# Decode attention over a long cache: softmax with a running maximum per head

## The chip, the cores and the metric

The kernel runs on one core of a Trainium2 chip. The metric is device time in microseconds (us) of one execution; the kernel before has a median of 1265.78 us over three runs (1265.28 to 1266.05).

## What is computed

One token is decoded. A gate `g` mixes the result of an attention block with that of a small MLP ("mixer"). The attention has 16 query heads on 8 key/value heads (so two query heads share each cache head), 65,536 cached positions and a head size of 256, all in bf16:

```python
scores = jnp.einsum("bhqd,bhkd->bhqk", q, k) * (Dh ** -0.5)
p = _softmax(scores, axis=-1)
o = jnp.einsum("bhqk,bhkd->bhqd", p, v)
return (lambda x, *d: x.transpose(*d))(o, 0, 2, 1, 3).reshape(B, Sq, Hq * Dh) @ wo
...
g = _sigmoid((x * gate_w).sum(-1, keepdims=True))
a = _A_ref(x, A_k_cache, A_v_cache, A_wq, A_wo)
b = _B_ref(x, B_w1, B_b1, B_w2, B_b2)
return g * a + (1 - g) * b
```

The two caches are 268 MB each. Each element of them is read once.

## The kernel before

**Tiling.** The 8 cache heads (`H`) are cut into 4 load pairs each (`PPH`), 32 in all (`NP`), numbered j = 0 to 31 here. A pair is one load of 8 MiB of K and one of 8 MiB of V, 16,384 positions, as 128 partitions x 128 positions x 256. A pair is worked through in 8 blocks (`BODY`) of 16 tiles of 128 positions (`NT`). K lives in a ring of one and a half pairs (`kring`), V in one buffer (`vbuf`). The last pair's K comes as two halves, its V as four pieces.

**DMA queue.** SP issues every large load, in order (L239 to L263): for each pair the K load, once half the transposes of the pair before are done (L242), then the V load, once the values of the pair before are done (`sem_pv`, L255), and in the first pair of heads 1 to 6 that head's output weights `wo_sb` (L263), once the projection with the old ones is done (L262). After the last pair the final two parts of `wo_sb` follow (L265 to L268).

**Keys (TensorE).** For each block `transposes` (L301) turns 16 tiles of K, read as 32-bit words, into four PSUM banks `kst`; DVE copies two of the banks to `ktT` (L572) and ACT the other two (L672). `scores` (L321) then multiplies each tile by the two queries in `qcur`: 32 small matmuls of two columns per block, into one of two PSUM banks of `sps`, by the parity of the block. TensorE runs the transposes of a block ahead of the scores of the block before it.

**Weights (ACT).** After each block of scores ACT takes the exponential of the bank's 32 columns, scaled, into `pT` (L661), with no maximum subtracted. TensorE waits for it before it overwrites the bank (L315).

**Values (TensorE).** After the eight blocks of a pair, `values` waits for the last exp (L348), adds the eight blocks of `pT`, summed over partitions by a matmul with ones, to the denominators (`acc[:, DENC:SELC]`, L350), then runs 128 matmuls of `pT` columns with `vbuf` (L361), which add to `acc[:, 0:DENC]` at rows 0, 32, 64 and 96 in turn. `acc` is one PSUM bank, and gathers over the four pairs of a head. In the last pair four projections (L345) and eight matmuls without a use (`spin(8)`, L337) stand ahead of L348, and the values from 112 on go through `late_values` (L382) into `sps[:, 0, 0:4]`.

**End of a head.** DVE copies `acc` out (`take`, L578), TensorE clears it and gathers the four row groups (`by_row`, L397), DVE scales by the reciprocal denominators and TensorE projects with `wo_sb` (L408).

**Mixer.** In pairs 0 to 13 DVE computes one tile of the MLP after its evacuations (L547 to L565, with a tanh on ACT, L678), and TensorE adds four small matmuls after the values (L471).

All order between engines is by semaphores written out by hand; each engine works through its own instructions in order.

Of the kernel before, what the change touches and what calls it, by code (L numbers as in the profile page):

```python
# [8 lines left out]
ALU = mybir.AluOpType  # L9
# [3 lines left out]
def bass_gated_mix__gqa_block_cached__mixer_token_mlp__decode_kernel(  # L13
# [57 lines left out]
    assert WG * NCG == DM  # L71

    scale = 1.0 / (DH ** 0.5)
    GC0 = 0.796875
    GC1 = 0.044677734375

# [15 lines left out]
    with ctx:  # L92
        def sb(shape, dt, name):
            return ctx.enter_context(nc.sbuf_tensor(name, shape, dt))

        def psum(shape, dt, name):
            return ctx.enter_context(nc.psum_tensor(name, shape, dt))
# [51 lines left out]
        sel = sb([P, REP], f32, "sel")  # L149
        zrow = sb([1, NACC], bf16, "zrow")  # L150
        rden = sb([P, REP], f32, "rden")
        densum = sb([P, REP], f32, "densum")
        rrow = sb([P, 1], f32, "rrow")
        b2_b = sb([1, 1], bf16, "b2_b")
# [15 lines left out]
        kst = psum([P, NB, 512], f32, "kst")  # L170
        kst_b = kst.bitcast(bf16)
        sps = psum([P, 2, 512], f32, "sps")
        acc = psum([P, 512], f32, "acc")
        prj = psum([P, 512], f32, "prj")

# [12 lines left out]
        sem_qk = new_sem("sem_qk")  # L188
        sem_exp = new_sem("sem_exp")
        sem_pv = new_sem("sem_pv")  # L190
        s_par = new_sem("s_par")
        s_hb = new_sem("s_hb")
        s_sel = new_sem("s_sel")
# [91 lines left out]
        def _(pe):  # L285
# [26 lines left out]

            def scores(k, c):
                par = k % 2
                pe.wait_ge(sem_exp, c + 1)  # L315
                for nt in range(NT):
                    b, ntl = divmod(nt, 4)
                    if k == BODY - 1 and ntl == 0:
                        pe.wait_ge(sem_ev[b], c + 2)
                    for dj in range(2):  # L320
                        ins = pe.matmul(sps[:, par, 2 * nt:2 * nt + 2],  # L321
                                        ktT[:, par, b, ntl * DH + dj:(ntl + 1) * DH:2],
                                        qcur[:, dj, :],
                                        start=(dj == 0), stop=(dj == 1))
                ins.then_inc(sem_qk, 1)
# [11 lines left out]
                    pe.matmul(kst[:, NB - 1, :], ones_sq[:, :], ktT[:, KTB - 1, 0, 0:512], start=True, stop=True)  # L337


            def values(j, c0, u16):  # L340
                with pe.If(j == NP - 1):
                    pe.wait_ge(s_mix, 1)
                    for q in range(NCG):
                        r = slice(32 * q, 32 * q + 1)
                        pe.matmul(prj[r, 0:WG], rest[r, :], brow[r, :], start=False, stop=True,  # L345
                                  skip_group_check=True)
                    spin(8)
                pe.wait_ge(sem_exp, c0 + (BODY + 2))  # L348
                for r in range(BODY):
                    pe.matmul(acc[:, DENC:SELC], ones_sq[:, :], pT[:, r, :],  # L350
                              start=False, stop=(r == BODY - 1), skip_group_check=True)

                def some(n0, n1, last=False):
                    if last:
                        piece_wait(n0)
                    else:
                        pe.wait_ge(sem_v, u16)
                    for n in range(n0, n1):
                        r, nt = divmod(n, NT)
                        o = 32 * (n % 4)  # L360
                        ins = pe.matmul(acc[o:o + REP, 0:DH], pT[:, r, 2 * nt:2 * nt + 2], vbuf[:, n, :],  # L361
                                        start=False, stop=False, skip_group_check=True)
# [14 lines left out]
            def late_values(n0, n1):  # L377
                for n in range(n0, n1):
                    r, nt = divmod(n, NT)
                    piece_wait(n)  # L380
                    for dj in range(2):
                        ins = pe.matmul(sps[:, 0, dj * REP:(dj + 1) * REP], vbuf[:, n, dj:DH:2],  # L382
                                        pT[:, r, 2 * nt:2 * nt + 2], start=False,
                                        stop=(n == NV - 1), skip_group_check=True)
                return ins
# [27 lines left out]

            def tail():
                pe.wait_ge(s_cp, H)
                by_d(sps[:, 0, 0:2 * REP])
# [66 lines left out]
        def _(vec):  # L483
            for b in range(0, NB, 2):
                vec.sem_inc(sem_ev[b], 1)
            vec.memset(xrem, 0.0)
            vec.memset(zrow[:, :], 0.0)
            vec.wait_ge(sem_ident, 1)
            vec.tensor_copy(identb, ident[0:3 * FT, 0:3 * FT]).then_inc(s_xrem, 1)
            vec.reduce_sum(sel[:, :], ident[:, :].rearrange("p (j n) -> p n j", j=4)[:, 0:REP, :], axis=AX.X)  # L490
# [102 lines left out]

            def finish_head(g):
                take(vec.snap(g * PPH + PPH, min_val=PPH, max_val=NP))
                vec.tensor_copy(qcur[:, :, :], qT[:, :, bass.ds(g * REP + REP, REP)])
# [32 lines left out]
            with nc.Fori(NC - NCPH, NC, BODY, engines=on) as c0:  # L629
                for k in range(BODY):  # L630
                    evacuate(k, c0 + k)
            take(1, s_early)
            vec.wait_ge(s_late, 1)
            by_head(sps[:, 0, 0:2 * REP])
# [5 lines left out]
        def _(act):  # L640
# [6 lines left out]
            act.sem_inc(sem_exp, 2)  # L647
# [18 lines left out]
            with nc.Fori(0, NP, 1, engines=OrderedEngineSet([act.engine])) as j:  # L666
                c0 = act.snap(j * BODY, min_val=0, max_val=NC)
                for k in range(BODY):
                    act.wait_ge(sem_qk, c0 + (k + 1))
                    for b in range(1, NB, 2):  # L670
                        act.wait_ge(sem_tr[b], c0 + (k + 1))
                        act.activation(ktT[:, k % KTB, b, :], kst_b[:, b, :], AF.Copy).then_inc(sem_ev[b], 1)  # L672
                    if k >= 1:
                        weights(k - 1, c0 + (k - 1))
                weights(BODY - 1, c0 + (BODY - 1))
                with act.If(j < FT):
                    act.wait_ge(s_u, j + 1)
                    act.activation(z_b[:, :], z_b[:, :], AF.Tanh).then_inc(s_tanh, 1)  # L678
# [32 lines left out]
```

## Time and profile before

| what | us |
|---|---|
| runs (median of 3) | 1265.78 |
| profiled execution, span | 1263.6 |
| TensorE matmul busy | 920.2 (73%) |
| ACT busy | 536.8 (42%) |
| DVE busy | 422.5 (33%) |
| share of 16 DMA engines in use | 99.7% |
| rate of the loads, mean | 431 GB/s |

The span is that of one profiled execution; the median of the runs stands 2.2 us above it. The costliest groups of instructions, each with its count, then its busy time, the mean of one in ns, and the idle time of its engine just before it with what ended it:

```profile
L672 ACT ACTIVATE ktT<-kst 128x1024 bf16<-128x1024 bf16 x512 | 498.5, 1021 | 668.1 <-PE kst L301 667.8
L301 PE MATMUL kst<-ident,kring 128*128 128x128 f32 x4096 | 554.2, 296 | 301.5 <-DMA kring<-in_A_k_cache_dram 289.8
L572 DVE COPY ktT<-kst 128x1024 bf16<-128x1024 bf16 x512 | 354.2, 692 | 762.8 <-PE kst L301 738.8
L321 PE MATMUL sps<-qcur,ktT 128*128 128x2 bf16 x8192 | 236.6, 163 | 1.1 <-issue 1.1
L361 PE MATMUL acc<-vbuf,pT 128*2 128x256 bf16 x4080 | 153.7, 323 | 3.4 <-issue 2.9
L661 ACT ACTIVATE pT<-sps 128x32 f32 x256 | 52.3, 204 | 16.2 <-PE sps L321 16.2
```

Matmuls overlap, so the mean length of one times their count is more than their busy time: the busy time is what the group took from the engine.

### The profile page before, as it was taken

The page shows a single profiled execution, that of the slowest core. Times are in us where ns is not written, and L with a number is a line of the kernel's source. Part 1 is how long each engine was busy: PE and PEld are TensorE (multiplying, and loading weights), DVE is VectorE, ACT ScalarE, POOL GpSimd, SP SyncE. Part 2 cuts the span into 40 slices and gives each one's busy share as a digit, 9 for nine tenths or more (in the row PEclk, how much of TensorE's full clock was granted, in tenths as well). Part 3 has the DMA queues.
Part 4 walks back from the last instruction along what each step waited for, and adds up shares of the span by engine and source line. Part 5 has one row for each costly group of instructions (what it writes and reads, how often), then busy time and mean ns, then how long its engine had stood idle before and what let it go on. Part 6 is the DMA issues. An engine that isn't in the chain of part 4 may idle for free.

```text
span 1263.6 us, 38848 instructions
## 1 busy us (share of the span) xinstructions
PE 920.2 (73%) x17112; PEld 864.9 (68%) x17114; DVE 422.5 (33%) x764; ACT 536.8 (42%) x788; POOL 0.9 (0%) x7
## 2 busy tenths in 40 slices
PE   2876678766778667786676876768767688676788
PEld 2766668766677666686666876658766578666687
DVE  2433344333344234343222332223323133332233
ACT  1543345533355433454333553335533355433455
POOL 0000000000000000000000000000000000000000
PEclk9887788787898887988788887789887888887899
DMA  9999999999999999999999999999999999999998
GB/s 416 430 430 432 434 432 434 436 434 436 432 434 432 432 434 436 425 436 436 438 432 429 432 432 434 436 436 434 432 434 432 440 434 432 432 434 434 432 426 369
DMA packets 11623, 544.39 MB, mean 431 GB/s; under 512 B 1369, under 2 KB 1628, under 8 KB 2908
## 3 DMA queue, kind: packets, MB, share of 16 engines
q1 hardware_dynamic: 11522, 544.22, 99.7%
q8 instruction: 8, 0.13, 0.0%
q10 hardware_dynamic: 90, 0.01, 0.0%
q14 instruction: 3, 0.02, 0.0%
HBM read 544.22 MB, written 0.00 MB: 431 GB/s over the span
## 4 chain that ended last, share of the span: by engine, by line
DMA 71%; PE 28%; issue 1%; SPq 0%; DVEq 0%; DVE 0%; ACT 0%; ACTq 0%
DMA kring<-in_A_k_cache_dram 68%; PE kst L301 23%; PE sps L321 4%; DMA wo_sb<-in_A_wo_dram 2%; PE acc L361 0%; SPq L236 0%; SPq L233 0%; SPq L268 0%; SPq L231 0%; SPq L228 0%; PE acc L350 0%; DVEq L92 0%; PE prj L408 0%; DVE out_row L637 0%; ACT pT L661 0%
## 5 line engine op out<-in xcount | busy, mean ns | idle before, releaser
L672 ACT ACTIVATE ktT<-kst 128x1024 bf16<-128x1024 bf16 x512 | 498.5, 1021 | 668.1 <-PE kst L301 667.8
L301 PE MATMUL kst<-ident,kring 128*128 128x128 f32 x4096 | 554.2, 296 | 301.5 <-DMA kring<-in_A_k_cache_dram 289.8
L301 PEld LDWEIGHTS kst<-ident,kring 128*128 128x128 f32 x4096 | 504.3, 154 | 311.4 <-issue 308.8
L572 DVE COPY ktT<-kst 128x1024 bf16<-128x1024 bf16 x512 | 354.2, 692 | 762.8 <-PE kst L301 738.8
L321 PEld LDWEIGHTS sps<-qcur,ktT 128*128 128x128 bf16 x8192 | 237.8, 96 | 3.9 <-issue 1.4
L321 PE MATMUL sps<-qcur,ktT 128*128 128x2 bf16 x8192 | 236.6, 163 | 1.1 <-issue 1.1
L361 PE MATMUL acc<-vbuf,pT 128*2 128x256 bf16 x4080 | 153.7, 323 | 3.4 <-issue 2.9
L361 PEld LDWEIGHTS acc<-vbuf,pT 128*2 128x2 bf16 x4080 | 111.5, 98 | 37.3 <-issue 3.4
L661 ACT ACTIVATE pT<-sps 128x32 f32 x256 | 52.3, 204 | 16.2 <-PE sps L321 16.2
L350 PE MATMUL acc<-pT,ones_sq 128*128 128x32 bf16 x256 | 11.7, 178 | 12.2 <-ACT pT L661 12.2
L350 PEld LDWEIGHTS acc<-pT,ones_sq 128*128 128x128 bf16 x256 | 8.6, 96 | 15.1 <-ACT pT L661 14.9
L578 DVE COPY accs<-acc 128x288 f32<-128x288 f32 x8 | 3.7, 458 | 40.1 <-PE acc L361 40.1
L678 ACT ACTIVATE z_b<-z_b 128x448 bf16<-128x448 bf16 x14 | 8.1, 576 | 20.7 <-DVE z_b L559 20.7
L397 PEld LDWEIGHTS acc<-sel,accs 128*64 128x64 f32 x112 | 10.8, 214 | 0.9
L397 PE MATMUL acc<-sel,accs 128*64 128x1 f32 x112 | 11.4, 261 | 0.0
L434 PE MATMUL acc<-vbuf 42*128 42x42 bf16 x1 | 0.2, 215 | 8.6 <-DMA b_b<-in_B_b_dram 8.6
L434 PEld LDWEIGHTS acc<-vbuf 42*128 42x128 bf16 x1 | 0.1, 102 | 8.7 <-DMA b_b<-in_B_b_dram 8.7
L408 PE MATMUL prj<-wo_sb,oTn 128*1 128x112 bf16 x128 | 3.5, 230 | 3.4 <-DVE oTn L603 2.9
L553 DVE TENSOR_TENSOR z_b<-wtmp,u_b 128x448 bf16<-128x448 bf16 x14 | 5.5, 393 | 1.0
L551 DVE TENSOR_TENSOR wtmp<-u_b 128x448 bf16<-128x448 bf16 x14 | 5.5, 392 | 1.0
L565 DVE TENSOR_TENSOR gu<-wtmp,z_b 128x448 bf16<-128x448 bf16 x14 | 5.5, 392 | 1.0
L557 DVE TENSOR_TENSOR z_b<-u_b,wtmp 128x448 bf16<-128x448 bf16 x14 | 5.5, 392 | 1.0
(89 smaller groups left out, 81.8 us busy)
## 6 DMA issues: line engine op xcount, KB each, us to landing
kring<-in_A_k_cache_dram SPq DMA_DIRECT2D x4, 4096.0 KB, 24.4
vbuf<-in_A_v_cache_dram SPq DMA_DIRECT2D x1, 6144.0 KB, 25.5
wo_sb<-in_A_wo_dram SPq DMA_DIRECT2D x7, 448.0 KB, 27.2
vbuf<-in_A_wq_dram SPq DMA_DIRECT2D x1, 3072.0 KB, 10.3
vbuf<-in_A_v_cache_dram SPq DMA_DIRECT2D x1, 1024.0 KB, 27.6
vbuf<-in_A_v_cache_dram SPq DMA_DIRECT2D x1, 768.0 KB, 28.7
vbuf<-in_A_wq_dram SPq DMA_DIRECT2D x1, 512.0 KB, 11.1
vbuf<-in_A_v_cache_dram SPq DMA_DIRECT2D x31, 29.5
```

Of the source, the lines that this page charges most:

```text
L301: ins = pe.transpose(kst[:, b, i * P:(i + 1) * P], kring_f[:, at + NT * (k % DC) + 4 * b + i, :], ident[:, :])
L321: ins = pe.matmul(sps[:, par, 2 * nt:2 * nt + 2], ktT[:, par, b, ntl * DH + dj:(ntl + 1) * DH:2], qcur[:, dj, :], start=(dj == 0), stop=(d ...
L350: pe.matmul(acc[:, DENC:SELC], ones_sq[:, :], pT[:, r, :], start=False, stop=(r == BODY - 1), skip_group_check=True)
L361: ins = pe.matmul(acc[o:o + REP, 0:DH], pT[:, r, 2 * nt:2 * nt + 2], vbuf[:, n, :], start=False, stop=False, skip_group_check=True)
L397: ins = pe.matmul(dst[hh * HP:(hh + 1) * HP, i:i + 1], accs[:, i:DH:2 * REP], sel[:, hh:hh + 1], start=False, stop=True, skip_group_check= ...
L551: vec.tensor_tensor(W, U, U, op=ALU.mult)
L553: vec.tensor_tensor(Z, W, U, op=ALU.mult)
L557: vec.tensor_tensor(Z, U, W, op=ALU.add)
L572: vec.tensor_copy(ktT[:, k % KTB, b, :], kst_b[:, b, :]).then_inc(sem_ev[b], 1)
L661: act.activation(pT[:, bass.ds(p0 + k % DC, 1), :].rearrange("p o n -> p (o n)"), sps[:, k % 2, 0:2 * NT], AF.Exp, scale=scale).then_inc(s ...
L672: act.activation(ktT[:, k % KTB, b, :], kst_b[:, b, :], AF.Copy).then_inc(sem_ev[b], 1)
L678: act.activation(z_b[:, :], z_b[:, :], AF.Tanh).then_inc(s_tanh, 1)
```

## The change

The softmax now subtracts a maximum, per query head, that runs along with the load pairs. The scores of all eight blocks of a pair go side by side into one PSUM bank (`scores_all`, 256 columns: block, tile, head), and the exps wait until the whole pair's scores are there. TensorE no longer waits for an exp between blocks.

Once per pair, between scores and values, this happens in order. DVE takes the maximum over the tiles of each partition and head (128x256 to 128x2) and the larger of that and the running maximum; TensorE transposes the 128x2 result to 2x128 (`mxT`); DVE takes the maximum of each row and sets it on a 2x2 diagonal; TensorE multiplies that with ones, which puts both maxima on all 128 partitions (`mxB`); DVE makes the bias `mneg` and the difference `mdif` between the old and the new maximum; ACT takes the exponential of the difference, `fade`, and then four exps, each of 64 columns (half of the blocks, one head), with `mneg` as bias, into `pT`; DVE meanwhile multiplies the denominators and the sums in `acc`, in PSUM, by `fade`; TensorE waits for both before it goes on to the denominators. At the end of a head the running maximum is set back to a very low value. The late values of the last pair go to the second bank of `sps`.

```diff
             def scores(k, c):
                 par = k % 2
-                pe.wait_ge(sem_exp, c + 1)
...
-                        ins = pe.matmul(sps[:, par, 2 * nt:2 * nt + 2],
+                        ins = pe.matmul(sps[:, 0, 2 * (NT * k + nt):2 * (NT * k + nt) + 2],
...
+            def maxima(j1):
+                pe.wait_ge(s_mcol, j1)
+                pe.transpose(mxT, mcol[:, :], ident[:, :]).then_inc(s_mT, 1)
+                pe.wait_ge(s_mdiag, j1)
+                pe.matmul(mxB, mones[:, :], mdiag[:, :], start=True, stop=True).then_inc(s_mB, 1)
...
             def values(j, c0, u16):
+                j1 = pe.snap(j + 1, min_val=1, max_val=NP)
+                maxima(j1)
                 with pe.If(j == NP - 1):
...
-                pe.wait_ge(sem_exp, c0 + (BODY + 2))
+                pe.wait_ge(s_acc, j1)
+                pe.wait_ge(sem_exp, j1)
...
+            vec.memset(mones[:, :], 1.0)
+            vec.memset(mrun[:, :], LOW)
...
+            def maxima(j1, c0):
+                vec.wait_ge(sem_qk, c0 + (BODY + 2))
+                vec.tensor_reduce(out=mcol[:, :], in_=scores_all.rearrange("p (n hh) -> p hh n", hh=REP),
+                                  axis=AX.X, op=ALU.max)
+                vec.drain()
+                vec.tensor_tensor(mcol[:, :], mcol[:, :], mrun[:, :], op=ALU.max).then_inc(s_mcol, 1)
+                vec.wait_ge(s_mT, j1)
+                vec.tensor_reduce(out=mrow[:, :], in_=mxT, axis=AX.X, op=ALU.max)
+                vec.drain()
+                vec.tensor_scalar(mdiag[:, :], ident[0:REP, 0:REP], mrow[:, :], None, op0=ALU.mult
+                                  ).then_inc(s_mdiag, 1)
+                vec.wait_ge(s_mB, j1)
+                vec.tensor_scalar(mneg[:, :], mxB, -scale, None, op0=ALU.mult)
+                vec.tensor_tensor(mdif[:, :], mrun[:, :], mxB, op=ALU.subtract).then_inc(s_mneg, 1)
+                vec.drain()
+                vec.tensor_copy(mrun[:, :], mxB)
+                vec.wait_ge(s_fade, j1)
+                vec.tensor_tensor(acc[:, DENC:SELC].rearrange("p (n hh) -> p n hh", hh=REP),
+                                  acc[:, DENC:SELC].rearrange("p (n hh) -> p n hh", hh=REP),
+                                  fade[:, :].rearrange("p (o hh) -> p o hh", o=1).broadcast_to((P, NT, REP)),
+                                  op=ALU.mult)
+                vec.tensor_tensor(fadej[:, :], fade[:, :], sel[:, :], op=ALU.mult)
+                vec.drain()
+                vec.reduce_sum(fader[:, :], fadej[:, :], axis=AX.X)
+                vec.drain()
+                vec.tensor_scalar(acc[:, 0:DENC], acc[:, 0:DENC], fader[:, :], None, op0=ALU.mult
+                                  ).then_inc(s_acc, 1)
...
                     for k in range(BODY):
                         evacuate(k, c0 + k)
+                    maxima(vec.snap(j + 1, min_val=1, max_val=NP), c0)
                     with vec.If(j < FT):
                         mixer(j)
...
-            def weights(k, c):
-                p0 = act.snap(pt_reg, min_val=0, max_val=DC)
-                act.wait_ge(sem_qk, c + 3)
-                act.activation(pT[:, bass.ds(p0 + k % DC, 1), :].rearrange("p o n -> p (o n)"),
-                               sps[:, k % 2, 0:2 * NT], AF.Exp, scale=scale).then_inc(sem_exp, 1)
-                if k == DC - 1:
-                    act.reg_sub(pt_reg, DC, pt_reg)
+            def weights(j1):
+                act.wait_ge(s_mneg, j1)
+                act.activation(fade[:, :], mdif[:, :], AF.Exp, scale=scale).then_inc(s_fade, 1)
+                for half in range(2):
+                    p0 = act.snap(pt_reg, min_val=0, max_val=DC)
+                    for hh in range(REP):
+                        ins = act.activation(pT[:, bass.ds(p0, DC), hh:2 * NT:REP],
+                                             scores_all.rearrange("p (a r n hh) -> p a hh r n", a=2, r=DC, hh=REP)[:, half, hh],
+                                             AF.Exp, bias=mneg[:, hh:hh + 1], scale=scale)
+                    if half == 0:
+                        act.reg_sub(pt_reg, DC, pt_reg)
+                ins.then_inc(sem_exp, 1)
...
-                    if k >= 1:
-                        weights(k - 1, c0 + (k - 1))
-                weights(BODY - 1, c0 + (BODY - 1))
+                weights(act.snap(j + 1, min_val=1, max_val=NP))
```

More of the change, by code (lines that the diff above doesn't have):

```diff
@@ L73, in bass_gated_mix__gqa_block_cached__mixer_token_mlp__decode_kernel @@
     scale = 1.0 / (DH ** 0.5)
+    LOW = -3.0e38
     GC0 = 0.796875
@@ L151, in bass_gated_mix__gqa_block_cached__mixer_token_mlp__decode_kernel @@
         rden = sb([P, REP], f32, "rden")
+        mrun = sb([P, REP], f32, "mrun")
+        mcol = sb([P, REP], f32, "mcol")
+        mrow = sb([REP, 1], f32, "mrow")
+        mdiag = sb([REP, REP], f32, "mdiag")
+        mones = sb([REP, P], f32, "mones")
+        mneg = sb([P, REP], f32, "mneg")
+        mdif = sb([P, REP], f32, "mdif")
+        fade = sb([P, REP], f32, "fade")
+        fadej = sb([P, REP], f32, "fadej")
+        fader = sb([P, 1], f32, "fader")
         densum = sb([P, REP], f32, "densum")
@@ L172, in bass_gated_mix__gqa_block_cached__mixer_token_mlp__decode_kernel @@
         sps = psum([P, 2, 512], f32, "sps")
+        SC = BODY * 2 * NT
+        scores_all = sps[:, 0, 0:SC]
+        mxT = sps[0:REP, 1, 0:P]
+        mxB = sps[:, 1, P:P + REP]
+        late = sps[:, 1, 2 * P:2 * P + 2 * REP]
+        assert SC <= 512
         acc = psum([P, 512], f32, "acc")
@@ L190, in bass_gated_mix__gqa_block_cached__mixer_token_mlp__decode_kernel @@
         sem_pv = new_sem("sem_pv")
+        s_mcol = new_sem("s_mcol")
+        s_mT = new_sem("s_mT")
+        s_mdiag = new_sem("s_mdiag")
+        s_mB = new_sem("s_mB")
+        s_mneg = new_sem("s_mneg")
+        s_fade = new_sem("s_fade")
+        s_acc = new_sem("s_acc")
         s_par = new_sem("s_par")
@@ L381, in late_values @@
                     for dj in range(2):
-                        ins = pe.matmul(sps[:, 0, dj * REP:(dj + 1) * REP], vbuf[:, n, dj:DH:2],
+                        ins = pe.matmul(late[:, dj * REP:(dj + 1) * REP], vbuf[:, n, dj:DH:2],
                                         pT[:, r, 2 * nt:2 * nt + 2], start=False,
@@ L415, in tail @@
                 pe.wait_ge(s_cp, H)
-                by_d(sps[:, 0, 0:2 * REP])
+                by_d(late)
                 late_values(NLATE, NV).then_inc(s_late, 1)
@@ L595, in finish_head @@
                 take(vec.snap(g * PPH + PPH, min_val=PPH, max_val=NP))
+                vec.memset(mrun[:, :], LOW)
                 vec.tensor_copy(qcur[:, :, :], qT[:, :, bass.ds(g * REP + REP, REP)])
@@ L628, in _ @@
             vec.tensor_scalar(brow, brow1, bcast[:, 2:3], None, op0=ALU.add).then_inc(s_mix, 1)
-            with nc.Fori(NC - NCPH, NC, BODY, engines=on) as c0:
+            with nc.Fori(NP - PPH, NP, 1, engines=on) as j:
+                c0 = vec.snap(j * BODY, min_val=0, max_val=NC)
                 for k in range(BODY):
                     evacuate(k, c0 + k)
+                maxima(vec.snap(j + 1, min_val=1, max_val=NP), c0)
             take(1, s_early)
             vec.wait_ge(s_late, 1)
-            by_head(sps[:, 0, 0:2 * REP])
+            by_head(late)
             vec.wait_ge(s_proj, H)
@@ L646, in _ @@
             act.dma_start(b2_b[:, :], B_b2.rearrange("(a n) -> a n", a=1)).then_inc(sem_misc, 16)
-            act.sem_inc(sem_exp, 2)
             for b in range(1, NB, 2):
```

## The prediction

> **What bounds the kernel now.** I read the page of the profile first, its DMA table and the chain that ended last, then the waits of the DMA queue and of TensorE, then the timeline of the last two load pairs.
>
> ```profile
> q1 hardware_dynamic: 11522, 544.22, 99.7%
> ...
> SPq L236 <- PE acc L361: 539.6, 31, 23.9
> ...
> PE kst L301 <- DMA kring<-in_A_k_cache_dram: 289.8, 31, 12.1
> ```
>
> The sixteen DMA engines are never free, and before each pair's transposes (L301) TensorE sits waiting for the K load, 289.8 us in 31 waits. So in the middle of the run compute has slack and the loads set the pace. How much slack: a V load is issued when the values of the pair before are done (SP's wait on L361), and must be issued before the K load ahead of it in the queue has landed. Taking the start of each pair's first transposes as the landing, the 30 V issues up to pair 30 come 9.01 to 12.06 us before it (63.58 against 72.59 is the least, 101.77 against 111.28 the next; mean 10.4). A queue started from nothing needs time: the first load is issued at 0.74, no byte moves by 1.6, the rate is full by 2.8, so I ask for 2.1 us of lead. 6.9 us (least) to 8.3 us (mean) may be lost between scores and values before a load is late.
>
> The end is different. First the chain of waits over the values of pair 30 (start, length, what), then the timeline of pair 31 (in brackets the idle time before):
>
> ```profile
> 1223.45 1.59 PE sps L321 x64
> ...
> 1225.42 0.36 PE acc L350 x8
> 1225.79 3.62 PE acc L361 x128
> ```
>
> ```profile
> 1230.82 3.83 PE L301 MATMUL kst<-ident,kring 128*128 128x128 f32 x32 [1.44 <-DMA kring<-in_A_k_cache_dram]
> ...
> 1241.02 1.96 PE L301 MATMUL kst<-ident,kring 128*128 128x128 f32 x16 [0.42 <-issue]
> ...
> 1250.57 1.74 PE L321 MATMUL sps<-qcur,ktT 128*128 128x2 bf16 x64
> ...
> 1254.13 0.35 PE L350 MATMUL acc<-pT,ones_sq 128*128 128x32 bf16 x8
> 1254.98 3.23 PE L361 MATMUL acc<-vbuf,pT 128*2 128x256 bf16 x112 [0.50 <-DMA vbuf<-in_A_v_cache_dram]
> ```
>
> Pair 30's scores end at 1225.04 and its values at 1229.41. Pair 31's K comes as two halves, so its first half is there 1.41 us later, and from 1230.82 TensorE works almost without a pause to the end: idle 0.42 at the second half, 0.50 at V. The chain of waits names the last wo load (landed 1261.12), but TensorE needs that only 0.19 us after it could have used it (first projection ends 1260.97, second starts 1261.16). Load and TensorE end together; nearly every us lost by TensorE after 1201.74 is a us of the total.
>
> Last, the granted clock, over two runs of pair values and one start of keys:
>
> ```profile
> 680.05:685.38 5.33, 5.33 (x131) 3.69 (x128) 0.00 (x0) 0.00 (x0) 0.00 (x0) 0.68 0.97 418
> ...
> 696.34:702.57 6.23, 6.23 (x39) 6.22 (x40) 2.47 (x4) 2.82 (x3) 0.00 (x0) 0.58 0.90 389
> ...
> 720.50:724.20 3.70, 3.70 (x134) 2.95 (x130) 0.00 (x0) 0.00 (x0) 0.00 (x0) 1.00 0.86 372
> ```
>
> The seventh number is the clock. The same 128 matmuls take 3.67 us at 1.00 and 5.33 at 0.68. In half-microsecond slices the clock is 0.50 from 602.55 to 605.95, and every fall lies a multiple of 3.41 us from this one: the grant is renewed per period. It fell here although only the two-column scores and a 0.39 us gap came before; the period 640.10 to 643.51, with 1.76 us of denominators and values (from 641.75), kept 1.00; the one from 599.13, with some 1.3 us of transposes and values beside the scores, lost it.
>
> **The change, part by part.** *Removed:* eight exps per pair on ACT (0.204 each) and TensorE's wait for them in the scores. A block of keys takes 1.81 (transposes) + 0.78 (scores) = 2.59 us, and TensorE is busy for all of it; ACT uses 2 x 1.02 + 0.20 = 2.24. So this gives nothing; if ACT were the bound it would give up to 0.2 per block.
>
> *Added before the first pair:* two small DVE memsets, 0.17 each by L486, in DVE's 0.53 us idle before L489: nothing, or 0.3 us that the loads cover.
>
> *Added between scores and values of every pair:* a round trip in which nothing overlaps. From the end of the scores:
> - DVE starts, 0.10 (ACT's L661 starts 0.15 after them, L578 0.06 after L361). Maximum of 128x256 from PSUM: no such row; between L580 (32 elements, 0.186) and L497 (448, 0.607) a straight line gives 0.41. Drain gap 0.07 (646.49 to 646.56), running maximum 0.164 (L591). Sum 0.75.
> - TensorE: hand-over 0.12 (L603 ends 648.38, load at 648.50), transpose of two columns 0.30 (L301). DVE: 0.04, row maximum of 128 elements 0.28 (same line), 0.07, diagonal 0.22 (L603). TensorE: 0.12, broadcast matmul 0.26 (L389). Sum 2.16.
> - DVE: 0.04, mneg 0.17 (L520), mdif 0.16 (L591). ACT: 0.03, fade 0.20 (L661). Sum 2.77.
> - DVE: 0.03, 128x32 of the sums 0.19 (L521), fadej 0.16, 0.07, its sum 0.15 (L490), 0.07, 128x256 of acc in PSUM 0.43 (L578 less 32 elements). TensorE 0.12. Sum 4.0 us.
>
> Beside the last step ACT does four exps of 64 columns; L661 and L672 (1021 for 1024) give 0.23 each, 0.92 in all, which ends before DVE's 1.1. The Trainium skill (ScalarE: Activation LUTs, What ACT_TABLE_LOAD costs) adds about 93 ns for a per-partition bias operand, which no row here has; by it, an estimate, the four would take up to 1.3 us and the sum grow by 0.2 us per exposed pair.
>
> Unknown are operations that read and write PSUM, tiny f32 matmuls alone, and waits against registers. Below: 3.4 us, if neighbours overlap as L503 and L504 do (0.37 apart, 0.44 long). Above: 6 us, with 0.61 for the first maximum, PSUM writes at twice L578, and the 0.2 "issue" gap of L547 at eight hand-overs. A gain is excluded: every step waits for the last. I take 4.0, since its rows are of near shapes. Queued behind DVE's waits are the mixer (14 pairs) and the next evacuations, behind ACT's tanh; none is needed before the next K lands, about 10 us after the old end of the values.
>
> *The clock.* TensorE now does next to nothing for 1.6 (scores) + 4.0 us, longer than a period, so the values start at half clock: 5.33 - 3.67 = 1.66 us more, by bounds 0 and 2.4 (32 transposes after a rest take up to 6.3, against 3.83 at full clock).
>
> *Pairs 0 to 29:* V issue later by 4.0 - 0.38 = 3.6, at most 5.3 with the clock. The spare is 6.9 or more. Nothing; a load is late from a round trip of about 6 us in pair 0, 7 to 9 elsewhere.
>
> *The end.* Pair 30's values end 3.6 + 1.66 = 5.3 later, at 1234.7. The first half of K has waited since 1230.82, so pair 31's transposes start 3.9 late; the 0.42 pause at the second half goes; its scores end 3.5 late (1255.8). Then the second round trip: 4.0, or TensorE's own work by which it must pass, broadcast done at 2.16 plus four projections and the eight spins (1252.24 to 1254.13, 1.89) = 4.05. Denominators 0.29 (641.75 to 642.04), the 112 matmuls 3.23, clock 1.66: the values end 9.2 after the scores. Before it was 1258.21 - 1252.31 = 5.9, with V's landing in it, which no longer waits. So 3.5 + 3.3 = 6.8 late. The rest as before, less the 0.19 wait for wo: **+6.6 us**. The span 1263.6 becomes 1270.2; the runs' median stands 2.2 above the span, so 1265.78 + 6.6 = **1272.4**.
>
> **Rivals.**
> 1. *The clock stays up over the round trip only:* 1272.4 - 2 x 1.66 = 1269.1. For it: the spins kept 1.00 at 1252 to 1254. Against: the fall at 602.55 after a far shorter gap. The Trainium skill (TensorE: Matmul & The Clock Gate, What's actually happening) states that the gate closes after at least one idle window of about 3.4 us; two small matmuls now split the gap, so by that rule it would stay open, and the estimate is this rival. The trace agrees on 3.41 us, not on idleness: TensorE was busy for most of the period before 602.55.
> 2. *Not slower: the shorter rest keeps the clock up throughout.* Pair 30's keys start after some 6 us of rest instead of 10.3; at clock 1.00 their first 32 transposes take 3.83 for 6.12, 2.3 less, and the values lose nothing: 1269.1 - 2.3 = 1266.8. It decides if the grant lasts through 6 us. For: those are the gaps that shrink. Against: after 648.9 (last work) it fell at 650.34.
> 3. *Loads late:* if the steps cost double, 8.0, the V issue moves 7.6 + 1.66 = 9.3, which exceeds the mean spare 8.3 by 1.0: 30 us over 30 pairs, and 8 more at the end: about 1310. For: no row of PSUM written by DVE. Against: four of five steps have a near row.
> 4. *All hidden, or the edit is not on the path:* wo's load ends the chain at 29.18 us. It would be 1265.8. Against: TensorE is 0.19 us behind it.
>
> **How the numbers follow.** A measurement tells 0.2% (2.5 us) from no change: 1268.3 and above is slower. Forecast 0.68, rival 1 0.11, rival 2 0.10, rival 3 0.07, rival 4 0.04. The forecast's own range: round trip 3.4 and no clock loss gives 2.4 us, 1268.2; 6 us and 2.4 of clock give 12, 1277.8. Slower: 0.68 + 0.11 + 0.07, less 0.02 for the forecast's low edge: 0.84. Faster 0.02, from rival 2's scatter; within 0.2%, 0.14. The range 1266.5 to 1277.8 takes in rivals 1 and 2 and leaves out rival 3, rival 4 and the forecast's edges.
>
> **What would show it.** About 4 us between the last L321 and the first denominator matmul in every pair; V issues 5 to 7 us ahead of landing and DMA still at 99%; K landings up to pair 30 at the old times; pair 31's first transposes near 1234.7 with no DMA wait; half clock in the values. Wrong if K lands later each pair (rival 3), if pair 31 starts at 1230.8, or if the values run at 1.00.

## The result, and the profile after

The changed kernel takes 1272.65 us (median of 5 runs, 1270.20 to 1273.32), the kernel before, run beside it, 1265.70 (5 runs, 1265.28 to 1266.05). The ratio is 1.0052, 95% interval 1.0040 to 1.0065: slower by 6.95 us. The profiled execution of after took 1273.0 us, its span is 1271.2 (before: 1263.6).

The page of after, its row of the load queue; then, from the views of waits, SP's wait for the end of the values and TensorE's for K (us in total, times, longest):

```profile
q1 hardware_dynamic: 11522, 544.22, 99.1%
```

```profile
SPq L260 <- PE acc L394: 677.0, 31, 24.8
```

```profile
PE kst L325 <- DMA kring<-in_A_k_cache_dram: 150.1, 30, 7.5
```

SP now waits 677.0 us for the end of the values where it waited 539.6, 4.4 more in each of 31 pairs: the V loads are issued about that much later (on the mean 5.8 us ahead of the next K landing, before 10.4). TensorE's wait for K fell from 289.8 to 150.1. DMA moves the same 544.22 MB and is nearly as full (99.1% of the longer span, before 99.7%). So over most of the run the change was paid out of TensorE's waiting time. The rows of TensorE give nearly the whole account (busy us, mean ns | idle us before, by what), first of after, then the one row of before that was not shown yet:

```profile
L325 PE MATMUL kst<-ident,kring 128*128 128x128 f32 x4096 | 561.5, 298 | 160.5 <-DMA kring<-in_A_k_cache_dram 150.1 <-issue 9.3
...
L394 PE MATMUL acc<-vbuf,pT 128*2 128x256 bf16 x4080 | 186.4, 368 | 0.0
L367 PE MATMUL sps<-mdiag,mones 2*128 2x2 f32 x64 | 15.2, 304 | 21.2 <-DVE mdiag L620 21.2
L383 PE MATMUL acc<-pT,ones_sq 128*128 128x32 bf16 x256 | 12.7, 190 | 51.0 <-DVE acc L636 51.0
...
L365 PE MATMUL sps<-ident,mcol 128*2 128x128 f32 x32 | 8.8, 276 | 24.1 <-DVE mcol L616 24.1
```

```profile
L350 PE MATMUL acc<-pT,ones_sq 128*128 128x32 bf16 x256 | 11.7, 178 | 12.2 <-ACT pT L661 12.2
```

Added: 69.3 us for the two small steps of TensorE with the waits ahead of them (L365, L367), 38.8 more waiting ahead of the denominators (L383 51.0, before 12.2), 32.7 for values that run at a lower clock (L394 186.4, before L361 153.7), 7.3 for the transposes: 148.1 us. The idle time before the transposes gave back 141.0 (301.5 to 160.5). What is left, 7.1, is about what the span grew (7.6); the smaller rows, some up and some down, nearly cancel.

Where that rest lies: the timeline of after from the last scores of pair 30 on, one line per group, in brackets the idle time before:

```profile
1223.04 1.74 PE L344 MATMUL sps<-qcur,ktT 128*128 128x2 bf16 x64
...
1228.70 0.40 PE L383 MATMUL acc<-pT,ones_sq 128*128 128x32 bf16 x8 [1.65 <-DVE acc L636]
1229.02 5.65 PE L394 MATMUL acc<-vbuf,pT 128*2 128x256 bf16 x128
1235.13 3.84 PE L325 MATMUL kst<-ident,kring 128*128 128x128 f32 x32 [0.46 <-issue]
...
1254.63 1.74 PE L344 MATMUL sps<-qcur,ktT 128*128 128x2 bf16 x64
1257.13 0.37 PE L365 MATMUL sps<-ident,mcol 128*2 128x128 f32 x1 [0.75 <-DVE mcol L616]
1258.16 0.58 PE L367 MATMUL sps<-mdiag,mones 2*128 2x2 f32 x2 [0.67 <-DVE mdiag L620]
1258.67 0.26 PE L377 MATMUL prj<-z_b,rest 1*1 1x112 bf16 x4
1258.87 3.59 PE L360 MATMUL kst<-ktT,ones_sq 128*128 128x512 bf16 x8
1262.25 0.42 PE L383 MATMUL acc<-pT,ones_sq 128*128 128x32 bf16 x8
1262.60 3.82 PE L394 MATMUL acc<-vbuf,pT 128*2 128x256 bf16 x112
```

Pair 31's transposes start at 1235.13 with no wait for DMA ahead of them; before, they started at 1230.82, after one. Its scores end at 1256.37 (1252.31 before), its values at 1266.42 (1258.21). Two steps of about 4 us: one comes over from pair 30, one is pair 31's own.

The granted clock (seventh number; the stretch, then its length, first), over the gap of a pair in mid-run, the end of its values, and both stretches of pair 31:

```profile
604.50:605.00 0.50, 0.08 (x1) 0.00 (x0) 0.29 (x3) 0.13 (x2) 0.00 (x0) 1.00 2.42 1049
605.00:605.50 0.50, 0.00 (x0) 0.00 (x0) 0.41 (x4) 0.50 (x4) 0.00 (x0) 0.58 0.00 0
...
611.50:612.00 0.50, 0.50 (x20) 0.33 (x16) 0.00 (x0) 0.00 (x0) 0.00 (x0) 0.59 1.51 655
```

```profile
1258.87:1262.25 3.38, 3.38 (x12) 1.18 (x9) 1.20 (x7) 1.07 (x5) 0.00 (x0) 0.50 0.29 108
1262.60:1266.42 3.82, 3.82 (x115) 2.69 (x112) 0.00 (x0) 0.00 (x0) 0.00 (x0) 0.84 0.00 0
1261.00:1270.00 9.00, 7.46 (x177) 4.99 (x175) 1.73 (x7) 0.52 (x2) 0.00 (x0) 0.84 0.00 0
```

The clock fell at about 605.1 and came back at about 611.9: two periods of 3.41 us. In pair 31 the eight spins ran at 0.50: with the four projections ahead of them they take 3.58 us (1258.67 to 1262.25), where before both took 1.88. The last row's 0 GB/s says that nothing is loaded any more after 1261.0.

The round trip itself in mid-run (scores end at 602.51), the timeline with DVE and ACT:

```profile
602.55 0.42 DVE L613 TENSOR_REDUCE mcol<-sps 128x2 f32<-128x256 f32 x1 [1.32 <-PE sps L344]
...
604.20 0.38 PE L367 MATMUL sps<-mdiag,mones 2*128 2x2 f32 x2 [0.66 <-DVE mdiag L620]
...
604.99 0.95 ACT L729 ACTIVATE pT<-sps,mneg 128x64 f32 x4
...
605.67 0.49 DVE L636 TENSOR_SCALAR acc<-acc,fader 128x256 f32<-128x256 f32 x1
606.22 0.29 PEld L383 LDWEIGHTS acc<-pT,ones_sq 128*128 128x128 bf16 x8 [1.73 <-DVE acc L636]
606.22 0.40 PE L383 MATMUL acc<-pT,ones_sq 128*128 128x32 bf16 x8 [1.64 <-DVE acc L636]
```

From 602.51 to 606.22 it is 3.71 us. DVE's last step ends at 606.16, the four exps at 605.94: the rescaling of `acc` is what the denominators wait for.

### The profile page after: what moved, and what is told of

It reads as the page before. It is cut to its first block, busy times and chain, and to the rows that moved or that the text cites. A ratio compares the mean times of both kernels' runs of the same rounds, so it can differ in the third digit from the quotient of the medians.

```text
span 1271.2 us, 39200 instructions
## 1 busy us (share of the span) xinstructions
PE 987.7 (78%) x17210; PEld 897.3 (71%) x17210; DVE 498.7 (39%) x1125; ACT 546.0 (43%) x692; POOL 0.9 (0%) x7
## 3 DMA queue, kind: packets, MB, share of 16 engines
q1 hardware_dynamic: 11522, 544.22, 99.1%
HBM read 544.22 MB, written 0.00 MB: 428 GB/s over the span
## 4 chain that ended last, share of the span: by engine, by line
DMA 68%; PE 31%; issue 1%; DVE 0%; SPq 0%; DVEq 0%
DMA kring<-in_A_k_cache_dram 68%; PE kst L325 25%; PE sps L344 5%; PE acc L394 1%; PE kst L360 0%; PE sps L367 0%; DVE mcol L613 0%; PE sps L415 0%; PE sps L365 0%; PE sps L422 0%; PE acc L383 0%; DVE mrow L618 0%; DVE acc L636 0%; DVE accs L641 0%; DVE mdiag L620 0%
## 5 line engine op out<-in xcount | busy, mean ns | idle before, releaser
L325 PE MATMUL kst<-ident,kring 128*128 128x128 f32 x4096 | 561.5, 298 | 160.5 <-DMA kring<-in_A_k_cache_dram 150.1
L325 PEld LDWEIGHTS kst<-ident,kring 128*128 128x128 f32 x4096 | 511.7, 155 | 170.8 <-issue 168.4
L344 PEld LDWEIGHTS sps<-qcur,ktT 128*128 128x128 bf16 x8192 | 237.7, 96 | 5.0 <-issue 2.5
L344 PE MATMUL sps<-qcur,ktT 128*128 128x2 bf16 x8192 | 236.6, 163 | 2.0 <-issue 2.0
L394 PE MATMUL acc<-vbuf,pT 128*2 128x256 bf16 x4080 | 186.4, 368 | 0.0
L394 PEld LDWEIGHTS acc<-vbuf,pT 128*2 128x2 bf16 x4080 | 120.4, 112 | 57.7
L383 PE MATMUL acc<-pT,ones_sq 128*128 128x32 bf16 x256 | 12.7, 190 | 51.0 <-DVE acc L636 51.0
L383 PEld LDWEIGHTS acc<-pT,ones_sq 128*128 128x128 bf16 x256 | 9.5, 106 | 54.1 <-DVE acc L636 53.6
L367 PEld LDWEIGHTS sps<-mdiag,mones 2*128 2x128 f32 x64 | 12.4, 240 | 27.5 <-DVE mdiag L620 27.5
L367 PE MATMUL sps<-mdiag,mones 2*128 2x2 f32 x64 | 15.2, 304 | 21.2 <-DVE mdiag L620 21.2
L613 DVE TENSOR_REDUCE mcol<-sps 128x2 f32<-128x256 f32 x32 | 13.6, 425 | 44.3 <-PE sps L344 44.3
L729 ACT ACTIVATE pT<-sps,mneg 128x64 f32 x128 | 30.5, 337 | 0.0
L365 PE MATMUL sps<-ident,mcol 128*2 128x128 f32 x32 | 8.8, 276 | 24.1 <-DVE mcol L616 24.1
L365 PEld LDWEIGHTS sps<-ident,mcol 128*2 128x2 f32 x32 | 2.6, 80 | 26.9 <-DVE mcol L616 26.9
L636 DVE TENSOR_SCALAR acc<-acc,fader 128x256 f32<-128x256 f32 x32 | 15.8, 492 | 2.5
L618 DVE TENSOR_REDUCE mrow<-sps 2x1 f32<-2x128 f32 x32 | 8.9, 278 | 11.8 <-PE sps L365 11.8
```

Of the source, the lines that this page charges most:

```text
L325: ins = pe.transpose(kst[:, b, i * P:(i + 1) * P], kring_f[:, at + NT * (k % DC) + 4 * b + i, :], ident[:, :])
L344: ins = pe.matmul(sps[:, 0, 2 * (NT * k + nt):2 * (NT * k + nt) + 2], ktT[:, par, b, ntl * DH + dj:(ntl + 1) * DH:2], qcur[:, dj, :], star ...
L365: pe.transpose(mxT, mcol[:, :], ident[:, :]).then_inc(s_mT, 1)
L367: pe.matmul(mxB, mones[:, :], mdiag[:, :], start=True, stop=True).then_inc(s_mB, 1)
L383: pe.matmul(acc[:, DENC:SELC], ones_sq[:, :], pT[:, r, :], start=False, stop=(r == BODY - 1), skip_group_check=True)
L613: vec.tensor_reduce(out=mcol[:, :], in_=scores_all.rearrange("p (n hh) -> p hh n", hh=REP), axis=AX.X, op=ALU.max)
```

## Experiments

All start from the changed kernel. The theory is the prediction's: the loss is two exposed round trips, in pairs 30 and 31, and half clock after them. The rival: each pair loses a little, through late loads or contention. A question beside it: whether the spins, and not the rest of the round trip, set the length of the second gap. Every ratio is against the kernel before, run on the same chip (medians 1265.56 to 1265.77).

### 1. The last two pairs without the round trip

`e3_last_two_free` skips the round trip in pairs 30 and 31: the exps take the maximum of pair 29, and nothing is rescaled. `e8_last_free` does so in pair 31 alone.

```diff
-                maxima(j1)
+                with pe.If(j < NP - 2):
+                    maxima(j1)
...
+                with vec.Else():
+                    vec.sem_inc(s_mneg, 1)
+                    vec.sem_inc(s_acc, 1)
...
             def weights(j1, c0):
+                act.wait_ge(sem_qk, c0 + (BODY + 2))
```

> Pairs 30 and 31 skip the round trip and use pair 29's maximum as the bias, with no rescaling there (a softmax is the same for any bias); pairs 0 to 29 keep it. Theory 'end': pair 30's denominators start some 1.2 us after its scores (four exps and one more), inside the 1.41 us that the first half of K leaves free; in pair 31 the eight spins cover the exps: 1265.7 to 1266.5 us, the time before. Rival 'loads': thirty pairs still issue V 5 us later, so the time stays near 1272. Rival 'round trip alone' agrees with 'end' here.

> Only pair 31 skips the round trip (bias and sums stay at pair 30's maximum); pairs 0 to 30 keep it. It splits the loss of the end in two. Theory 'end' with the prediction's terms: pair 30's round trip and half clock put pair 31's scores 3.5 to 4 us late; of that the waits for V (0.5) and wo (0.2) take up some: 1268.6 to 1269.6 us. Rival 'one of the two': if pair 31 alone made the loss it is 1266 or less, if pair 30 alone, 1272.

Measured: e3 1265.70 (11 runs), ratio 1.0000 (0.9991 to 1.0009); e8 1269.15 (6 runs), 1.0031 (1.0018 to 1.0043). The 30 round trips that stay in e3 cost nothing that can be measured; pair 30's costs 3.4 us (1269.15 against the 1265.77 of before, beside it) and pair 31's 3.5 (1272.65 less 1269.15). So the loss is that of the last two pairs, and the rival falls. The starts of pair 31 and its values in the timelines of e3 and then of e8:

```profile
1232.74 3.84 PE L325 MATMUL kst<-ident,kring 128*128 128x128 f32 x32 [0.21 <-issue]
...
1255.93 0.35 PE L384 MATMUL acc<-pT,ones_sq 128*128 128x32 bf16 x8
1256.21 3.23 PE L395 MATMUL acc<-vbuf,pT 128*2 128x256 bf16 x112
```

```profile
1235.76 3.84 PE L325 MATMUL kst<-ident,kring 128*128 128x128 f32 x32 [0.41 <-issue]
...
1258.94 0.35 PE L384 MATMUL acc<-pT,ones_sq 128*128 128x32 bf16 x8
1259.22 3.23 PE L395 MATMUL acc<-vbuf,pT 128*2 128x256 bf16 x112
```

Even e3 starts pair 31 1.92 us later than before (1232.74 against 1230.82): its four exps stay behind the scores, and pair 30's values still take 5.33 us at the lower clock. Its values of pair 31 start 1.23 later than before's (1254.98), and its span is only 0.6 longer (1264.2): the end has some slack of its own, such as the waits for V and `wo` that before shows there, and a round trip behind the last loads costs what goes beyond it.

In e8 pair 31 starts 0.6 us later than in after (1235.76 against 1235.13), but its values then take 3.23 at full clock and end at 1262.45, where after ends at 1266.42.

### 2. The spins and the clock

`e1_no_spins` takes the eight spins out of the last pair. `e2_filled_gaps` does the opposite: it puts spins into the round trip of every pair, so that TensorE has something dense to do at each of its three waits.

```diff
-                    spin(8)
```

```diff
             def maxima(j1):
+                spin(3)
                 pe.wait_ge(s_mcol, j1)
...
+                spin(2)
                 pe.wait_ge(s_mdiag, j1)
...
-                    spin(8)
+                    spin(6)
+                with pe.Else():
+                    spin(7)
```

> The eight matmuls without a use in the last pair are taken out; nothing that is computed changes. Theory 'end' (the whole loss is in pairs 30 and 31: two round trips and a half clock): in the changed kernel these eight ran at half clock, 1258.87 to 1262.25, while DVE was done with acc at 1260.33, so the denominators start about 1.8 us earlier; but the values then run at half clock for longer, up to 1.7 us more. Sum -1.8 to 0: 1270.9 to 1272.7 us. Rival 'round trip alone' (the clock costs nothing): at full clock the eight end with DVE, so no change: 1272.6. Rival 'loads' (loads come later in the middle of the run): no change, 1272.6.

> TensorE fills its waits of the round trip with matmuls without a use, in every pair (three before the transpose, two before the broadcast, seven before the denominators; six instead of eight in the last pair); nothing that is computed changes. Theory 'end': the clock stays at 1.00 through the values; pair 30's values take 3.67 instead of 5.65 us (-2.0), pair 31's gap 4.1 instead of 5.9 (-1.8), its values 3.2 instead of 3.8 (-0.6): about 1268.2 us, and the runs lie closer together than 1270.2 to 1273.3. Rival 'round trip alone': the gaps are as long as before, 1272.6 or a little more. Rival 'loads': V issues move forward by some 2 us in every pair, but if loads were lost the gain would be spread over all pairs, seen as earlier K landings before pair 30.

Measured: e1 1271.64 (5 runs), 1.0049 (1.0035 to 1.0062); e2 1268.99 (8 runs), 1.0023 (1.0013 to 1.0034). The end of e1 in its timeline:

```profile
1260.01 0.40 PE L382 MATMUL acc<-pT,ones_sq 128*128 128x32 bf16 x8 [1.45 <-DVE acc L635]
1260.34 4.68 PE L393 MATMUL acc<-vbuf,pT 128*2 128x256 bf16 x112
```

Without spins the denominators start 4.01 us after the scores (1256.00) and not 5.88, and they wait for DVE's `acc`: the spins at half clock did set the second gap. But the values then take 4.68 and not 3.82, since more of them fall into the slow period. Net 1.0 us in the trace (9.02 from scores to the end of the values against 10.05), and the medians, 1.0 apart, lie within the scatter of both; the time alone would not have shown it.

In e2 the values hold the full clock, here in mid-run:

```profile
605.33:609.00 3.67, 3.66 (x131) 2.89 (x128) 0.00 (x0) 0.00 (x0) 0.00 (x0) 1.00 0.95 411
```

The time is 3.7 us below after's, of the 6.95 lost: about half the loss goes when the gaps are filled. In mid-run the round trip is as long as it was (3.71), and only the values are faster. Two things missed: in the profiled run (1270.69, slower than the median) the last spins of pairs 30 and 31 still met a slow period (seven took 3.17 us, six 2.74) and made pair 30's gap longer (4.96 from scores to denominators, 3.92 in after), and the spread of the runs, 1267.91 to 1272.45, was not smaller than after's.

### 3. How far the loads were from being late

Experiment 1 says that the other 30 round trips of 3.7 us are hidden; it doesn't say how nearly they were not. Three kernels make the round trip of pairs 0 to 29 longer by DVE sums whose result nothing uses (`e9_delay_two` 1.35 us, `e5_delay_four` 2.70, `e6_delay_eight` 5.4), and leave the last two pairs as they are. `e10_late_tensor` makes TensorE late instead, behind the end of the values, where the V load has already been released.

```diff
+            def delay():
+                for _ in range(4):
+                    vec.reduce_sum(idle[:, :], hbT[:, :], axis=AX.X)
+                    vec.drain()
...
+                slow()
                 vec.tensor_scalar(acc[:, 0:DENC], acc[:, 0:DENC], fader[:, :], None, op0=ALU.mult
                                   ).then_inc(s_acc, 1)
```

```diff
+                with pe.If(j < NP - 2):
+                    spin(14)
```

> Two DVE sums instead of four in the round trip of pairs 0 to 29, 1.35 us. V is then issued some 3.1 to 7.7 us before the K load ahead of it lands, against 4.5 to 9.1 in the changed kernel, where the K landings stayed 38.7 apart, and 2.2 to 6.4 with four sums, where some 20 us were lost. Theory 'lead' (a V load needs a certain lead, between the two): losses only in the few pairs below about 4 us: 1273 to 1279. If any lead above 2.6 us is enough (as the run with eight sums reads), 1272.6.

> Four DVE sums without a use (0.61 us each and a gap, 2.7 us in all) stand in the round trip of pairs 0 to 29 only. In the changed kernel V is issued 4.5 to 9.1 us before the K load ahead of it lands; this makes it 1.8 to 6.4. Theory 'end' (loads have room for it): 1272.6 us, up to 1275 if the 2.1 us that I ask for a queue's start are needed in full. Rival 'loads' (the middle is already paying): 30 x 2.7 = 81 us more, 1353.

> As the run with four, with eight sums, 5.4 us in pairs 0 to 29. V is then issued from 0.9 us after to 3.7 us before the K load ahead lands. Theory 'end': the room is gone and the loads become late by the queue's start less the mean lead of 0.4, 0.9 to 1.7 us a pair: 1300 to 1325 us, with K landings further apart than 38.7 us. If the loads still have room it stays at 1273; rival 'loads': 30 x 5.4 = 162 more, 1435.

> Fourteen matmuls without a use stand behind the values of pairs 0 to 29 (3.0 us at full clock), after the signal that lets V be issued; nothing is added to the round trip. It tells the late V issue apart from a late TensorE in the run with four sums, which delayed both by 3 us. Theory 'lead' (the V issue is what costs): 1272.6 or a little less, since the clock may stay up into the next keys. Rival 'TensorE late' (the next pair's transposes start late and push the K issue): near the 1292.7 of the run with four sums.

| kernel | delay, us | median (runs) | ratio, interval |
|---|---|---|---|
| after | 0 | 1272.65 (5) | 1.0052, 1.0040 to 1.0065 |
| e9 | 1.35 | 1275.24 (4) | 1.0083, 1.0066 to 1.0100 |
| e5 | 2.70 | 1292.73 (4) | 1.0226, 1.0206 to 1.0245 |
| e6 | 5.4 | 1302.63 (4) | 1.0280, 1.0258 to 1.0303 |
| e10 | 3.19, TensorE | 1271.60 (4) | 1.0043, 1.0026 to 1.0060 |

e5 was a clear miss: nearly nothing was expected, and it lost 20 us more than after. e6 and e9 came out within what was expected of them. The lines to read are a V issue, the next K landing (transposes that waited for DMA), and the same again a pair later. First after, then e5:

```profile
104.99 0.33 SPq L260 DMA_DIRECT2D vbuf<-in_A_v_cache_dram  x1
111.01 4.31 PE L325 MATMUL kst<-ident,kring 128*128 128x128 f32 x19 [6.01 <-DMA kring<-in_A_k_cache_dram]
...
149.72 6.04 PE L325 MATMUL kst<-ident,kring 128*128 128x128 f32 x32 [4.54 <-DMA kring<-in_A_k_cache_dram]
```

```profile
107.67 0.33 SPq L261 DMA_DIRECT2D vbuf<-in_A_v_cache_dram  x1
111.21 3.84 PE L326 MATMUL kst<-ident,kring 128*128 128x128 f32 x32 [3.55 <-DMA kring<-in_A_k_cache_dram]
...
151.25 6.64 PE L326 MATMUL kst<-ident,kring 128*128 128x128 f32 x32 [6.14 <-DMA kring<-in_A_k_cache_dram]
```

In after V is issued 6.02 us ahead of the landing, and the next K lands 38.71 after the last. In e5 the lead is 3.54, and the next K takes 40.04: 1.3 us lost, though the lead was still positive, and though TensorE was waiting for DMA. Over all pairs of the profiled runs whose transposes waited for K (30 in after, 30 in e9, 26 in e5): in after the least lead is 4.52 and K lands every 38.70 (39.83 where a `wo` part lies between), but for one landing that came 0.53 late behind a lead of 5.52; in e9 the least is 4.08 and the landings keep that beat too; in e5 the leads are 2.2 to 6.4, and the worst pairs (leads 2.23 and 2.30) lose 2.8 and 2.6. The loss is no clean function of the lead: in e5 a pair at 3.80 lost nothing and one at 4.05 lost 1.3. e9's median is still 2.6 above after's, though its profiled run (1273.84) lost no pair; where its other runs lost it was not recorded.

In e10 TensorE is busy for 3.19 us more in a mid-run pair, longer than e5's delay, and the median is not above after's. That speaks for the late issue of V and against a late TensorE, with one reserve: the spins also keep the clock up (0.873 over the run, in after 0.829), the next transposes are faster, and V is issued earlier than in after (mean lead 7.0 against 5.8). e5 itself says the same more directly, since its transposes still waited for DMA. (e10's profiled run, 1276.74, is its slowest: there one pair's lead was 3.69 and it lost 1.8.)

### 4. The round trip under the last blocks

`e4_max_of_six` takes the maximum of the earlier pairs and of blocks 0 to 5 of this one only, and lets the round trip run while TensorE is at blocks 6 and 7; the scores of those two blocks are left out of the maximum that is subtracted (sums and denominators share it). Only the four exps stay behind the scores. `e7_max_of_six_filled` adds five spins in the gap that stays (four in place of eight in the last pair).

```diff
                 for k in range(1, BODY):
                     transposes(k, c0 + k, *where)
+                    if k == BODY - 1:
+                        pe.wait_ge(s_mcol, j1)
+                        pe.transpose(mxT, mcol[:, :], ident[:, :]).then_inc(s_mT, 1)
                     scores(k - 1, c0 + k - 1)
+                pe.wait_ge(s_mdiag, j1)
+                pe.matmul(mxB, mones[:, :], mdiag[:, :], start=True, stop=True).then_inc(s_mB, 1)
                 scores(BODY - 1, c0 + BODY - 1)
```

> The maximum is taken over blocks 0 to 5 of each pair and the pairs before (blocks 6 and 7 are left out of the maximum, not of the softmax), and the round trip goes on while TensorE works on blocks 6 and 7; only the four exps stay behind the scores. Theory 'end': about 1.1 us between scores and denominators plus 0.5 us for the transpose and the broadcast among the keys; pair 30 fits nearly into its 1.41 us, pair 31's exps lie beside the spins: 1265.8 to 1267 us. Rival 'loads' or any cost of the added work itself (acc rescaled in PSUM, ACT's strided exps): stays above 1269.

> The maximum over blocks 0 to 5 as before, and five matmuls without a use between scores and denominators in every pair (four instead of eight in the last). Theory 'end': the clock now stays up in the short gap, which took half clock in some runs (1265.4 to 1269.3 without them), and pair 31's values start with V's landing as in the kernel before: 1265.5 to 1266.3 us, the runs closer together. Rival 'the clock is not the cause of the spread': 1266.8, spread as before.

Measured: e4 1266.79 (11 runs, 1265.37 to 1269.29), ratio 1.0007 (0.9998 to 1.0016); e7 1266.05 (11 runs, 1265.28 to 1267.32), 1.0002 (0.9993 to 1.0011). The end of pair 30 in e7's timeline:

```profile
1225.38 1.24 PE L365 MATMUL kst<-ktT,ones_sq 128*128 128x512 bf16 x5
1226.76 0.35 PE L384 MATMUL acc<-pT,ones_sq 128*128 128x32 bf16 x8
1227.04 3.66 PE L395 MATMUL acc<-vbuf,pT 128*2 128x256 bf16 x128
1231.33 3.84 PE L325 MATMUL kst<-ident,kring 128*128 128x128 f32 x32 [0.62 <-DMA kring<-in_A_k_cache_dram]
```

Pair 31's transposes wait for DMA again, as in before, and start 0.5 us after theirs. In e4's profiled run pair 30's values still take 5.33 us, here 3.66. Such a maximum costs nothing that can be told here if its round trip lies beside matmuls that TensorE does anyway. But it is a weaker one: nothing bounds the exps of blocks 6 and 7 when their scores lie far above all earlier ones, and a maximum over all eight blocks was not tried in this place. No version was faster than the kernel before, whose last pairs are set by the loads.

## Why the prediction was right

The forecast was 1272.4 us, +6.6; measured 1272.65, +6.95. The mechanism is the one that was forecast: 30 hidden round trips, two exposed ones, and half clock after them. That the number came so close is partly luck. In the profiled runs the span grew by 7.6 us, 1.0 more than forecast; the 2.2 us that the forecast adds from span to median are 1.8 in after's profiled run (1273.0 less 1271.2), and that run lies 0.35 above the median. And two terms were wrong in opposite directions, as the list shows. By its steps:

- **Removed exps and wait: nothing.** Right: the scores keep TensorE busy for 236.6 us before (L321) and after (L344), and the account above needs no term for them.
- **Round trip 4.0 us.** 3.71 in mid-run, 3.92 in pair 30, where the broadcast matmul ran at half clock (0.58 for 0.38). The near rows were good: first maximum 0.42 (0.41 forecast), DVE on `acc` in PSUM 0.49 (0.43), row maximum 0.28 (0.28). The broadcast matmul came as two records, 0.38 (0.26). Most hand-overs were shorter than the 0.12 assumed. One exp with bias has a mean of 337 ns, 107 above the 230 of the rows without one; the Trainium skill (ScalarE: Activation LUTs, What ACT_TABLE_LOAD costs) says about 93 for that operand, and the trace agrees for one alone. But the four follow each other in 0.95, not in the 1.3 that the prediction summed from that figure: each begins before the one ahead of it is over, and they end ahead of DVE.
- **Pairs 0 to 29: nothing.** Right in the time (e3), wrong in the margin. "I ask for 2.1 us of lead" and "a load is late from a round trip of about 6 us in pair 0, 7 to 9 elsewhere" came from the start of an empty queue. e9 and e5 put the need near 4 us: with a least lead of 4.52 the change had used up nearly all of the room, and rival 3 was nearer than its 0.07 said. Its mechanism is real (e5, e6), and 2.7 us more are enough for it; at 1.35 us more (e9) the median rose by 2.6, with no late pair in the profiled run. Pair 0, which the prediction took for the tightest, kept its lead (9.09, before 9.01): in before its values pause for 2.94 us anyway.
- **Pair 30 over to pair 31:** V issue 1234.72, forecast 1234.7. Transposes 1235.13, forecast 1234.7; the 0.46 before them is "issue"; why it shows here is open, perhaps because there is no wait for DMA any more in which it could be done.
- **The clock, 1.66 for each of the exposed values.** Pair 30's cost 1.98 (5.65 against 3.67): they ran slow for their first 4.1 us (1229.0 to 1233.1), and not for 3.3.
- **The second gap, 4.05: the term that was mis-sized.** It was 5.88. The term took the four projections and the spins at 1.89, their time at full clock, although the same working has the clock at half for the values right behind them; at 0.50 they take 3.58. What the spins lost, the 112 values partly did not: 3.82, where 3.23 + 1.66 = 4.89 was forecast. Clock in all: 1.98 and 0.59 in the two pairs' values and 1.69 in the spins and projections, 4.3 against 3.3.
- **wo's load no longer ends anything:** right, 0 GB/s after 1261.0.

Of the rivals, 1 (the clock stays up) fell in after and came about in e2, where the gaps are filled. The Trainium skill (TensorE: Matmul & The Clock Gate, What's actually happening) has the gate close after at least one idle window of about 3.4 us. The trace agrees on the length of the period, not on idleness: in the one that ended near 605.1 there were 0.85 us of two-column scores and two small steps of matmuls, and the clock fell all the same; that sparse work does not count as busy would explain it. The same section of the Trainium skill calls the window free-running. The traces agree: in after, e1 and e8, whose code is the same up to the values of pair 30, the clock fell 1.5, 1.2 and 2.1 us after that pair's scores, and its values took 5.65, 5.48 and 5.97 us. That this makes the wider spread of the runs (3.1 us after, 0.8 before) is argued and not shown. Rival 2 (shorter rests keep the clock up) fell: the transposes' busy time rose from 554.2 to 561.5. Rival 4 fell with the wait for DMA ahead of pair 31.

## What to carry to other kernels

In a kernel that waits for its loads, a serial round trip per load is free only as long as the next load is still issued in time; behind the last loads it costs what goes beyond the slack there: count the pairs at the end that have nothing left to hide behind, and price the clock after the gap as well as the gap. Filler work put into a gap must be priced at the clock that the gap leaves. Moving the round trip beside the last blocks of the same pair took away nearly all of the cost (e4, e7), for a maximum that leaves those blocks out.

## What the hardware showed that was not expected

- An 8 MiB load wanted to be issued about 4 us ahead of the landing of the one before it: at 4.08 and more in e9, and 4.52 and more in after, no pair was late but one in after, by 0.53 us; between 2.2 and 4.1 in e5 pairs lost up to 2.8 us. Why pairs at the same lead lost different amounts is open; the trace has no row for the single DMA engines.
- After the gap the clock stayed at 0.50 for two periods (about 605.1 to 611.9, and 1226.3 to 1233.1). In mid-run dense matmuls filled 2.3 us of the first of them (from 606.22 to its end near 608.5) and did not bring the clock back, while in the kernel before a period with 1.76 us of them kept the 1.00 that it had.
